# Rank-20 second phase of an attention and mixture-of-experts kernel: weight preparation rearranged

## The chip, the cores and the metric

The kernel runs on one core of one Trainium2 chip. The metric is the device time of one execution in microseconds, taken as the median of the runs. Five engines work side by side, each through its own instructions in order: PE (TensorE, the matrix multiplications), DVE (VectorE), ACT (ScalarE), POOL (GpSimd) and SP (SyncE, which here only issues transfers). Transfers issued by SP and by POOL run on the DMA engines.

## The reference

A linear attention with a complex decay makes `x`, and a dense mixture of four experts follows on it:

```python
for t in range(S):                     # S = 768; batch 4, heads 8, head_dim 48
    S_re, S_im = ar*S_re - ai*S_im + k_t v_t^T, ar*S_im + ai*S_re
    y[:, :, t] = q_t @ S_re
x = y as [3072, 384]
p = domain_probs / (domain_probs.sum(-1) + 1e-9)
for e in range(4):                     # w1[e]: 384x1024, w2[e]: 1024x384
    out += p[:, e:e+1] * (relu(x @ w1[e]) @ w2[e])
```

All of it is float32. The kernel reaches float32 accuracy on PE by splitting each operand into a high part and a low part (`hi`, `lo`, in the type fp32r) and taking three products, hi·hi, lo·hi and hi·lo.

## The kernel before

**First phase.** It does the attention in 12 groups of 256 tokens and, one group behind, the first two experts on them (`moe1`, lines 209 to 229). A step over two blocks of 128 hidden features does the first layer into `ph`, takes `hh` on ACT (L219) and `hl` on DVE (L220), and runs the second layer of the step before (`po`, L229). The attention's result goes to memory (`y_d`), the sum over the first two experts to `acc_d`. In the last group there is no attention left beside the matrix work; there the second phase's first operands are prepared.

**Second phase.** It does experts 2 and 3 (E1 = 2) on all tokens, with a first layer in a scheme of rank 20: a product of a 4x3 by a 3x2 grid of blocks in 20 block products in place of 24. There are 8 rounds R, four for each expert; a round takes 768 tokens, as two token blocks u of 384 in the scheme's columns. A round has two units h = 0 and 1, each for 4 of the expert's 8 feature blocks. A unit (`unit`, from the table `UNIT`) runs 20 products of three matmuls each (`M` rows, into PSUM banks `pb0` to `pb4`), with copies on ACT (`C`), sums on DVE (`D`) and the hidden activations' high and low parts (`H` on ACT, `L` on DVE). `SN` holds copies that those steps keep. At the 8 places marked `F` the unit calls `fill`, which runs nine matmuls of the second layer (`l2`, into `pob0` to `pob2`) for a token block that was finished before; so a full unit has 60 + 72 = 132 matmuls. At the places marked `B` it calls `bg(n)`, which takes n steps from the list `side`, in which the preparation of later operands waits. Each engine runs its instructions in the order in which they are written in the second phase (`pin`, `held`), the sums on POOL excepted; up to the first unit and for POOL's sums, the scheduler sets the order.

**Preparing x for a round** (`prep_x`): SP loads six blocks into `Z` slots 0 to 5 (`load_x2`, L1012), 12 sums are formed in `Z` slots 0 to 10 on POOL (`pool`, L895), the first five of them into slots 6 to 10, and each of 16 operands is split into `xh` on ACT (L886) and `xl` on DVE (L889 and L892).

**Preparing four feature blocks of an expert's weights** (`prep_w`): four loads of the first-layer weights into a staging area (L954), 15 sums of 128-column blocks on DVE (L889), splits into `shi` and `slo` tiles and `ext`, and for the second-layer weights a POOL transfer that writes the high part (L992), an ACT copy with sign turned and a POOL transfer that adds the weight onto it (L994). `late_w` says where this happens: the first half of expert 2 before the first unit, staged in `SN` with sums in `ACC`; the second half in unit (0, 0), and the two halves of expert 3 in the units (1, 0) and (4, 0), all three staged in `Z` slots 0 to 3, with sums in `Z` from slot 4 on. `side` holds the weights first, and the loads of x for the next round after them. At the end of a unit h = 0 all of `side` is emptied (`drain`).

`ACC` has two halves, one for each token block u; `acc_load` (L1085) brings the sum so far, L892 adds the round's result, and a POOL transfer (L1117) stores it, or an SP transfer (L1115) writes the output for the last expert.

Of the kernel before, what the change touches and what calls it, by code (L numbers as in the profile page):

```python
# [8 lines left out]
F32 = mybir.dt.float32  # L9
F32R = mybir.dt.float32r  # L10
AF = mybir.ActivationFunctionType
ALU = mybir.AluOpType
# [4 lines left out]
HD = H * D  # L17
NT = B * S
E, F = 4, 1024
P = 128  # L20
NJ = HD // P
# [6 lines left out]
FE = F // P  # L28
E1 = 2
# [20 lines left out]
TB2 = 384  # L50
C2 = TB2 // P
NB2 = NT // (2 * TB2)
# [46 lines left out]
def fast_path(ctx, tc, qkP, aP, vP, probsP, w, out, flag):  # L99
    nc = tc.nc  # L100
# [10 lines left out]
                            base=32, channel_multiplier=1)  # L111
# [24 lines left out]
    wts = {}  # L136
# [121 lines left out]
    mo = MoE()  # L258

    with ExitStack() as c1:  # L260
# [4 lines left out]
        def tmp(name):  # L265
# [6 lines left out]
                                base=0, channel_multiplier=-1)  # L272
# [70 lines left out]
        last = {}  # L343
# [66 lines left out]

        def pick(g, nm, X, dst, s, w):
            n = 4 if w == C else 3
# [367 lines left out]
        x = {}  # L780
# [79 lines left out]
    with ExitStack() as c2:  # L860
        fin = c2.enter_context(tc.tile_pool(name="fin", bufs=1))
        ps_b = c2.enter_context(tc.tile_pool(name="ps_b", bufs=1, space=PSUM))
        acc2_d = [dram.tile([P, HD], F32, name=f"acc2_d{c}") for c in range(NT // P)]
        NR2 = (E - E1) * NB2
        Z = fin.tile([P, 11 * TB2], F32, name="Z")
        SN = fin.tile([P, 7 * TB2], F32, name="SN")
        ACC = fin.tile([P, 2 * C2 * HD], F32, name="ACC")
        X = [tuple(fin.tile([P, TB2], F32R, name=f"x{nm}{n}") for nm in ("h", "l")) for n in range(16)]
        static, quads = {}, {}
        held = {"on": False}  # L870
        side, freed, ready = [], set(), set()
# [7 lines left out]
        def pin(ins):  # L879
            return tc.keep_in_program_order(ins) if held["on"] else ins  # L880
# [4 lines left out]
        def act(dst, src, fn=AF.Copy, scale=1.0):  # L885
            return pin(nc.scalar.activation(dst, src, fn, scale=scale))  # L886
# [27 lines left out]

        def step(*ops, need=None, on=None):
            f = tt if on is None else on

            def run():
                for o in ops:
                    f(*o)  # L920
            return ["sum" if on is None else "pool", need, run, None]
# [23 lines left out]
                second()  # L945
                n -= 1

        def prep_w(e, h, base, raw, sums):
            i = e * FE + 4 * h
            raw = raw.rearrange("p (f k c) -> p f k c", f=4, k=NJ)  # L950
            s = sums.rearrange("p (n c) -> p n c", c=P)

            def load(u):
                pin(nc.sync.dma_start(raw[:, u].rearrange("p k c -> p (k c)"), w[i + u][:, :HD]))  # L954

            hi, lo = ([slot(nm, base + n) for n in range(5)] for nm in ("hi", "lo"))
            ext = fin.tile([P, 4 * P], F32R, tag="ext", name=f"ext{i}", bufs=3)
            ops = {}
            for n, r in enumerate((12, 9, 7, 15, 6, 8, 1, 16, 14, 13, 17, 4, 3, 2, 10, 19, 11, 5)):
                ops[r] = hi[n // 6][:, cut(n % 6)], lo[n // 6][:, cut(n % 6)]  # L960
            ops[18], ops[0] = ((ext[:, cut(n)], ext[:, cut(2 + n)]) for n in range(2))
            quads[e, h] = ops

            def blocks(x, n):
                return x.rearrange("p (n c) -> p n c", c=P)[:, n]

            def a(f, k):
                return raw[:, f - 1, k - 1]

            def n(lo_, hi_):  # L970
                return s[:, lo_:hi_]

            add, sub = ALU.add, ALU.subtract
            out = [step(*[(u,) for u in range(4)], on=load), ["gap", None, 2, None],
                   step((n(0, 4), raw[:, :, 1], raw[:, :, 0], sub)),
                   step((n(10, 12), raw[:, 2, :2], raw[:, 3, :2], add), (s[:, 8], a(1, 3), a(4, 3), add)),
                   step((s[:, 9], a(2, 3), a(3, 3), add), (n(4, 6), n(0, 2), raw[:, :2, 2], add)),
                   step((n(6, 8), n(0, 2), n(8, 10), add), (s[:, 5], s[:, 5], a(4, 3), sub)),
                   step((s[:, 12], a(1, 2), a(2, 1), add), (s[:, 8], s[:, 12], s[:, 8], add),
                        (s[:, 9], s[:, 12], s[:, 9], sub)),  # L980
                   step((s[:, 10], s[:, 6], s[:, 10], sub), (s[:, 11], s[:, 7], s[:, 11], add)),
                   step((s[:, 13], a(3, 1), a(4, 2), add), (s[:, 14], a(3, 1), a(1, 2), sub))]
            for src, q, lim in ((n(0, 6), 0, slice(0, 6)), (n(6, 12), 1, slice(0, 6)), (n(12, 15), 2, slice(0, 3)),
                                (raw[:, 2, 0::2], 2, slice(3, 5)), (a(2, 1), 2, 5)):
                out.append(split(blocks(hi[q], lim), blocks(lo[q], lim), src))
            out.append(split(blocks(ext, slice(0, 2)), blocks(ext, slice(2, 4)), raw[:, 3, 1:3], mark=("w", e, h)))
            for u in range(4):
                d_hi, d_lo = (x[3 + u // 2][:, u % 2 * HD:(u % 2 + 1) * HD] for x in (hi, lo))
                wts[i + u] = d_hi, d_lo

                def minus(d_hi=d_hi, d_lo=d_lo, k=i + u):
                    nc.gpsimd.dma_start(d_hi, w[k][:, HD:])  # L992
                    act(d_lo, d_hi.bitcast(F32), scale=-1.0)
                    nc.gpsimd.dma_start(d_lo, w[k][:, HD:], accum_op=ALU.add)  # L994
                    if k == i + 3:
                        ready.add(("w2", e, h))
                out.append(["act", None, minus, None])
            return out

        def drain():  # L1000
            while side:
                bg(len(side))
# [157 lines left out]
        held["on"] = True  # L1160
        for R in range(NR2):
            for h in range(2):
                if h == 1 or R > 0:
                    acc_load(R if h == 1 else R - 1, 1 - h)
                if (R, h) in late_w:
                    e, q, base = late_w[R, h]
                    side += prep_w(e, q, base, Z[:, :4 * HD], Z[:, 4 * HD:4 * HD + 15 * P])
                if h == 0 and R + 1 < NR2:
                    todo_x = prep_x(R + 1)
                    side += todo_x[:2]  # L1170
                elif R + 1 < NR2:
                    freed.clear()
                    side += todo_x[2:]
# [205 lines left out]
```

## Time and profile before

| | |
|---|---|
| Median of 3 runs | 1015.28 us (1014.23 to 1017.97) |
| The profiled execution | 1014.26 us, of it 1012.6 us span |
| Granted TensorE clock, mean | 0.984 |
| PE busy | 958.2 us (95%) |
| DVE busy | 748.3 us (74%) |
| ACT busy | 479.3 us (47%) |
| POOL busy | 181.4 us (18%) |
| Second phase, first to last matmul | 604.46 to 1006.3 us |

A row of the timeline has the start, the length, the engine, line, operation, output and inputs, and in brackets how long the engine had been idle before it and what ended that. The matmuls of a row overlap a little, so the pace is read from their starts. In a table of windows each engine's column is its busy time in that stretch with the number of instructions in brackets, and PEclk is the mean granted clock. The profile has no chain of waits for this kernel, so the windows and the timeline take its place.

### The profile page before, as it was taken

The numbers are of one execution on the slowest core, as the hardware profiler recorded it, in microseconds if no ns is written. First come the engines' busy times: TensorE is split into PE (matmuls) and PEld (weight loads), VectorE is DVE, ScalarE is ACT, GpSimd is POOL, SyncE is SP. The second block draws the span as 40 slices with busy tenths as digits, with TensorE's granted clock in tenths as the row PEclk, the third lists the DMA queues.
The fourth block names the chain that finished last, engine by engine and source line by source line (L and its number), as shares of the span: only waits on it lengthen the run. The fifth ranks groups of instructions, "written<-read, shape, count | busy, mean of one in ns | idle before, by whom it ended". The sixth has DMA issues, their size and how long they took to land.

```text
span 1012.6 us, 17537 instructions
## 1 busy us (share of the span) xinstructions
PE 958.2 (95%) x6717; PEld 930.9 (92%) x6717; DVE 748.3 (74%) x1594; ACT 479.3 (47%) x952; POOL 181.4 (18%) x218
## 2 busy tenths in 40 slices
PE   5899999999999999999999897988999979999997
PEld 2799999999999999999999897888999969999997
DVE  7888989898988889798832656867575768475743
ACT  7756525546365363645422436544454535354430
POOL 6030000000000000000000433525333334223000
PEclk9999999999999999999999899998999999999999
DMA  9585277394784745648361345333313242231112
GB/s 300 177 179 127 76 188 162 100 217 100 181 181 136 188 124 150 173 110 198 85 133 48 94 109 129 109 80 95 119 51 107 78 107 74 94 94 49 48 47 74
DMA packets 107053, 123.82 MB, mean 122 GB/s; under 512 B 7440, under 2 KB 94528, under 8 KB 106960
## 3 DMA queue, kind: packets, MB, share of 16 engines
q1 hardware_dynamic: 95472, 95.69, 34.2%
q0 software_dynamic: 11488, 26.93, 11.7%
q8 instruction: 55, 0.90, 0.4%
q14 instruction: 38, 0.31, 0.1%
HBM read 81.96 MB, written 40.62 MB: 121 GB/s over the span
## 4 chain that ended last, share of the span: by engine, by line


## 5 line engine op out<-in xcount | busy, mean ns | idle before, releaser
L883 PE MATMUL pob<-shi,hid 128*128 128x384 f32 x528 | 149.7, 338 | 0.0
L229 PE MATMUL po<-whi,hh 128*128 128x384 f32 x384 | 130.0, 339 | 1.1 <-ACT hh L219 1.1
L229 PE MATMUL po<-whi,hl 128*128 128x384 f32 x384 | 125.3, 341 | 5.4 <-DVE hl L220 5.4
L219 ACT ACTIVATE hh<-ph 128x512 fp32r<-128x512 f32 x96 | 57.1, 595 | 153.4 <-PE ph L209 148.8
L229 PE MATMUL po<-wlo,hh 128*128 128x384 f32 x384 | 129.3, 337 | 0.0
L895 POOL TENSOR_TENSOR Z<-Z 128x384 f32<-128x384 f32 x96 | 105.4, 1122 | 123.0 <-DMA Z<-y_d 65.6
L883 PE MATMUL pb<-xh,shi 128*128 128x384 f32 x291 | 99.7, 344 | 22.8 <-ACT SN L886 13.5
L220 DVE SCALAR_TENSOR_TENSOR hl<-ph,hh 128x512 fp32r<-128x512 f32 x96 | 66.0, 688 | 53.7 <-ACT hh L219 53.0
L209 PE MATMUL ph<-xha,whi 128*128 128x256 f32 x576 | 104.3, 287 | 1.2 <-ACT xha L196 1.2
L209 PE MATMUL ph<-xha,wlo 128*128 128x256 f32 x576 | 101.8, 284 | 0.0
L209 PE MATMUL ph<-xla,whi 128*128 128x256 f32 x576 | 101.2, 284 | 0.4 <-DVE xla L198 0.4
L883 PEld LDWEIGHTS pob<-shi,hid 128*128 128x128 f32 x528 | 98.5, 192 | 0.0
L889 DVE TENSOR_TENSOR xl<-Z,xh 128x384 fp32r<-128x384 f32 x104 | 70.2, 705 | 37.7 <-ACT xh L886 32.1
L883 PE MATMUL pb<-xh,slo 128*128 128x384 f32 x288 | 97.9, 340 | 0.0
L883 PE MATMUL pb<-xl,shi 128*128 128x384 f32 x288 | 97.8, 340 | 0.0
L883 PE MATMUL pob<-slo,hid 128*128 128x384 f32 x264 | 89.3, 338 | 0.0
L209 PEld LDWEIGHTS ph<-xha,whi 128*128 128x128 f32 x576 | 86.5, 191 | 2.5 <-ACT xha L196 1.5
L209 PEld LDWEIGHTS ph<-xla,whi 128*128 128x128 f32 x576 | 82.9, 191 | 0.6 <-DVE xla L198 0.6
L209 PEld LDWEIGHTS ph<-xha,wlo 128*128 128x128 f32 x576 | 83.2, 191 | 0.2 <-issue 0.2
L883 PEld LDWEIGHTS pb<-xh,shi 128*128 128x128 f32 x291 | 55.5, 191 | 27.0 <-ACT SN L886 14.4
L229 PEld LDWEIGHTS po<-whi,hl 128*128 128x128 f32 x384 | 71.3, 189 | 7.0 <-DVE hl L220 6.9
L886 ACT ACTIVATE xh<-Z 128x384 fp32r<-128x384 f32 x128 | 60.6, 516 | 35.5 <-POOL Z L895 33.7
(217 smaller groups left out, 2069.1 us busy)
## 6 DMA issues: line engine op xcount, KB each, us to landing
qk<-qkP SPq DMA_DIRECT2D x24, 384.0 KB, 7.0
acc_d<-acc POOLq DMA_DIRECT2D x24, 384.0 KB, 4.8
ACC<-acc_d SPq DMA_DIRECT2D x48, 192.0 KB, 3.1
A<-aP SPq DMA_DIRECT2D x22, 384.0 KB, 8.0
Z<-y_d SPq DMA_DIRECT2D x16, 384.0 KB, 4.7
q_d<-Q SPq DMA_DIRECT2D x12, 387.0 KB, 3.9
Qst<-q_d SPq DMA_DIRECT2D x12, 387.0 KB, 5.8
v<-vP SPq DMA_DIRECT2D x24, 192.0 KB, 2.6
```

The source lines that it names most:

```text
L209: ins = nc.tensor.matmul(ph[:, u, :], wt[:, j * P:(j + 1) * P], xt[:, j, :], start=(n == 0), stop=(n == 3 * NJ - 1))
L219: wts["hh"] = nc.scalar.activation(hh, ph, AF.Relu)
L220: nc.vector.scalar_tensor_tensor(hl, ph, 0.0, hh, op0=ALU.max, op1=ALU.subtract)
L229: nc.tensor.matmul(po[t], ht[:, u, t * P:(t + 1) * P], wt[:, HD:], start=(i % FE == 0 and n == 0), stop=(i % FE == FE - 1 and n == 2))
L883: return tc.keep_in_program_order(nc.tensor.matmul(*args, **kw))
L886: return pin(nc.scalar.activation(dst, src, fn, scale=scale))
L889: pin(nc.vector.tensor_tensor(dst, x, y, op=op))
L895: nc.gpsimd.tensor_tensor(dst, x, y, op=op)
```

## The change

There is a tile of its own, `RX` (384 columns), and the staging areas are new. `prep_w` now returns its loads, its sums and splits, one step with the four W2 transfers that write the high parts ("casts"), and the four steps for their low parts ("tail") apart.

- Both halves of expert 2 are prepared before the first unit. The first is staged in the first half of `ACC` and in `RX`, the second in `SN`. The sums of both are formed in `Z` slots 6 to 10.
- The x sums of round 0 run on DVE in place of POOL.
- In units (1, 0) and (4, 0) the weights of expert 3 are staged in the first half of `ACC` and in `RX`, with sums in `Z` slots 6 to 10. Their loads are issued as the unit begins. The loads of x for the next round stand ahead of the weights in `side`, the five first x sums behind them, the tail in the unit h = 1.
- One second-layer step of the first token block moves from the end of the second unit to place 6 of the first, so the store of that block comes a step sooner.

```diff
-        def prep_w(e, h, base, raw, sums):
+        def prep_w(e, h, base, rows, last):
...
+            s = Z[:, 6 * TB2:].rearrange("p (n c) -> p n c", c=P)
...
             def a(f, k):
-                return raw[:, f - 1, k - 1]
+                return last[:, k - 1] if f == 4 else rows[:, f - 1, k - 1]
...
+            def loads():
+                for u in range(4):
+                    pin(nc.sync.dma_start(rows[:, u] if u < 3 else last,
+                                          w[i + u][:, :HD].rearrange("p (k c) -> p k c", k=NJ)))
...
-                def minus(d_hi=d_hi, d_lo=d_lo, k=i + u):
-                    nc.gpsimd.dma_start(d_hi, w[k][:, HD:])
-                    act(d_lo, d_hi.bitcast(F32), scale=-1.0)
-                    nc.gpsimd.dma_start(d_lo, w[k][:, HD:], accum_op=ALU.add)
...
+            def cast(k):
+                nc.gpsimd.dma_start(wts[k][0], w[k][:, HD:])
+
+            def rest(k):
+                act(wts[k][1], wts[k][0].bitcast(F32), scale=-1.0)
+                nc.gpsimd.dma_start(wts[k][1], w[k][:, HD:], accum_op=ALU.add)
...
             def g(*ops):
-                return step(*ops, on=pool)
+                return step(*ops, on=pool if R else None)
...
-        late_w = {(0, 0): (E1, 1, 5), (1, 0): (E1 + 1, 0, 10), (NB2, 0): (E1 + 1, 1, 0)}
+        half = C2 * HD
+        jobs = [prep_w(E1, h, 5 * h, x[:, :half], y) for h, x, y in ((0, ACC, RX), (1, SN, SN[:, half:half + HD]))]
         freed.update(range(16))
         side += prep_x(0)
-        drain()
-        side += prep_w(E1, 0, 0, SN[:, :4 * HD], ACC[:, :15 * P])
+        side[0][2]()
+        for job in jobs:
+            job[0]()
+        side.pop(0)
+        for _, main, casts, tail in jobs:
+            side += main + casts + tail
         drain()
...
+                if h == 0:
+                    side += todo_x[:1]
+                    tail = []
+                    if R in (1, NB2):
+                        loads, main, casts, tail = prep_w(E1 + 1, *((0, 10) if R == 1 else (1, 0)), ACC[:, :half], RX)
+                        loads()
+                        side += [["gap", None, 1, None]] + main + casts
+                    side += todo_x[1:2]
+                else:
+                    side += tail
...
-                def fill(k, first=(R == 0 and h == 0)):
-                    if not first:
+                def fill(k, u=2 * R + h):
+                    if u == 0 and k == 0:
+                        mo.flush()
+                    elif u > 1 or (u, k) == (0, 6) or (u == 1 and k < FE - 1):
                         l2()
-                    elif k == 0:
-                        mo.flush()
```

What this does to the order, at the three places that the prediction speaks of. First DVE in the last group of the first phase, between the low parts `hl_0` and `hl_1` of its first two steps, before:

```order
L220 SCALAR_TENSOR_TENSOR hl_0_6504<-ph_0_6484,hh_0_6503 128x512
L889 TENSOR_TENSOR xl_6825<-Z,xh_6824 128x384
L889 TENSOR_TENSOR xl_6827<-Z,xh_6826 128x384
L889 TENSOR_TENSOR xl_6831<-Z,xh_6830 128x384
L889 TENSOR_TENSOR ACC<-SN 128x128
L889 TENSOR_TENSOR xl_6843<-Z,xh_6842 128x384
L889 TENSOR_TENSOR xl_6821<-Z,xh_6820 128x384
L889 TENSOR_TENSOR ACC<-SN 128x128 x2
```

and after:

```order
L220 SCALAR_TENSOR_TENSOR hl_0_6504<-ph_0_6484,hh_0_6503 128x512
L890 TENSOR_TENSOR Z<-Z 128x384 x2
L890 TENSOR_TENSOR xl_6826<-Z,xh_6825 128x384
L890 TENSOR_TENSOR xl_6828<-Z,xh_6827 128x384
L890 TENSOR_TENSOR Z<-Z 128x384 x3
L890 TENSOR_TENSOR xl_6832<-Z,xh_6831 128x384
L890 TENSOR_TENSOR xl_6844<-Z,xh_6843 128x384
L893 SCALAR_TENSOR_TENSOR xl_6834<-Z,xh_6833 128x384
L890 TENSOR_TENSOR Z<-Z 128x384
L890 TENSOR_TENSOR xl_6822<-Z,xh_6821 128x384
L893 SCALAR_TENSOR_TENSOR xl_6816<-Z,xh_6815 128x384
L220 SCALAR_TENSOR_TENSOR hl_1_6545<-ph_1_6525,hh_1_6544 128x512
```

Weight sums (`ACC<-SN`) have left this stretch, and six x sums (`Z<-Z`) have come into it.

Second, ACT from the last high part of the first phase (`hh_7`) into the first unit, before; `acc` takes the last result of the first phase out of `po`, `pb<-pb` and `SN<-pb` are the unit's first copies:

```order
L219 ACTIVATE hh_7_6760<-ph_7_6741 128x512
L886 ACTIVATE pb_6960<-pb_6956 128x384
L682 ACTIVATE acc_1_6979<-po_4_0_6669,pr 128x384
L682 ACTIVATE acc_1_6979<-po_4_1_6670,pr 128x384
L886 ACTIVATE SN<-pb_6956 128x384
```

and after:

```order
L219 ACTIVATE hh_7_6760<-ph_7_6741 128x512
L887 ACTIVATE shi_6856<-Z 128x768
L887 ACTIVATE shi_6857<-Z 128x768
L887 ACTIVATE shi_6858<-Z 128x384
L887 ACTIVATE shi_6858<-SN 128x256
L887 ACTIVATE shi_6858<-SN 128x128
L682 ACTIVATE acc_1_7024<-po_4_0_6669,pr 128x384
L887 ACTIVATE slo_6864<-shi_6859 128x384
L682 ACTIVATE acc_1_7024<-po_4_1_6670,pr 128x384
L887 ACTIVATE slo_6864<-shi_6859 128x384
L887 ACTIVATE slo_6865<-shi_6860 128x384 x2
L887 ACTIVATE pb_7005<-pb_7001 128x384
```

The unit's first copy now stands behind the `acc` copies and four copies of the second weight half.

Third, POOL in round 1, from the store of the token block before to the x sums for round 2, before:

```order
L992 DMA shi_7356<-w 128x384 x2
L992 DMA shi_7357<-w 128x384 x2
L1117 DMA acc_d_6788<-ACC 128x384
L994 DMA slo_7361<-w 128x384 x2
L1117 DMA acc_d_6789<-ACC 128x384
L994 DMA slo_7362<-w 128x384
L1117 DMA acc_d_6790<-ACC 128x384
L994 DMA slo_7362<-w 128x384
L895 TENSOR_TENSOR Z<-Z 128x384 x12
```

and after:

```order
L993 DMA shi_7359<-w 128x384 x2
L993 DMA shi_7360<-w 128x384 x2
L896 TENSOR_TENSOR Z<-Z 128x384 x6
L1121 DMA acc_d_6788<-ACC 128x384
L1121 DMA acc_d_6789<-ACC 128x384
L1121 DMA acc_d_6790<-ACC 128x384
L997 DMA slo_7364<-w 128x384 x2
L997 DMA slo_7365<-w 128x384 x2
L896 TENSOR_TENSOR Z<-Z 128x384 x6
```

Six of the twelve sums now stand ahead of the block's store, in the unit h = 0, as they do in the rounds without weights. In round 4 the rows have the same shape.

More of the change, by code (lines that the diff above doesn't have):

```diff
@@ L867, in fast_path @@
         ACC = fin.tile([P, 2 * C2 * HD], F32, name="ACC")
+        RX = fin.tile([P, TB2], F32, name="RX")
         X = [tuple(fin.tile([P, TB2], F32R, name=f"x{nm}{n}") for nm in ("h", "l")) for n in range(16)]
@@ L946, in bg @@
                 n -= 1
-        def prep_w(e, h, base, raw, sums):
+        def prep_w(e, h, base, rows, last):
             i = e * FE + 4 * h
[L950 to L954, printed above, removed]
             hi, lo = ([slot(nm, base + n) for n in range(5)] for nm in ("hi", "lo"))
             ext = fin.tile([P, 4 * P], F32R, tag="ext", name=f"ext{i}", bufs=3)
+            rows = rows.rearrange("p (f k c) -> p f k c", f=3, k=NJ)
+            last = last.rearrange("p (k c) -> p k c", k=NJ)
+            s = Z[:, 6 * TB2:].rearrange("p (n c) -> p n c", c=P)
             ops = {}
@@ L967, in a @@
             def a(f, k):
-                return raw[:, f - 1, k - 1]
+                return last[:, k - 1] if f == 4 else rows[:, f - 1, k - 1]
             def n(lo_, hi_):
                 return s[:, lo_:hi_]
+            def loads():
+                for u in range(4):
+                    pin(nc.sync.dma_start(rows[:, u] if u < 3 else last,
+                                          w[i + u][:, :HD].rearrange("p (k c) -> p k c", k=NJ)))
             add, sub = ALU.add, ALU.subtract
[L974 to L977, printed above, removed]
+            out = [step((n(0, 3), rows[:, :, 1], rows[:, :, 0], sub), (s[:, 3], a(4, 2), a(4, 1), sub)),
+                   step((n(10, 12), rows[:, 2, :2], last[:, :2], add), (s[:, 8], a(1, 3), a(4, 3), add)),
+                   step((s[:, 9], a(2, 3), a(3, 3), add), (n(4, 6), n(0, 2), rows[:, :2, 2], add)),
                    step((n(6, 8), n(0, 2), n(8, 10), add), (s[:, 5], s[:, 5], a(4, 3), sub)),
@@ L983, in prep_w @@
             for src, q, lim in ((n(0, 6), 0, slice(0, 6)), (n(6, 12), 1, slice(0, 6)), (n(12, 15), 2, slice(0, 3)),
-                                (raw[:, 2, 0::2], 2, slice(3, 5)), (a(2, 1), 2, 5)):
+                                (rows[:, 2, 0::2], 2, slice(3, 5)), (a(2, 1), 2, 5)):
                 out.append(split(blocks(hi[q], lim), blocks(lo[q], lim), src))
-            out.append(split(blocks(ext, slice(0, 2)), blocks(ext, slice(2, 4)), raw[:, 3, 1:3], mark=("w", e, h)))
+            out.append(split(blocks(ext, slice(0, 2)), blocks(ext, slice(2, 4)), last[:, 1:], mark=("w", e, h)))
             for u in range(4):
-                d_hi, d_lo = (x[3 + u // 2][:, u % 2 * HD:(u % 2 + 1) * HD] for x in (hi, lo))
-                wts[i + u] = d_hi, d_lo
-                def minus(d_hi=d_hi, d_lo=d_lo, k=i + u):
-                    nc.gpsimd.dma_start(d_hi, w[k][:, HD:])
-                    act(d_lo, d_hi.bitcast(F32), scale=-1.0)
-                    nc.gpsimd.dma_start(d_lo, w[k][:, HD:], accum_op=ALU.add)
[L995 to L998, printed above, removed]
+                wts[i + u] = tuple(x[3 + u // 2][:, u % 2 * HD:(u % 2 + 1) * HD] for x in (hi, lo))
+            def cast(k):
[3 more added lines that the diff above has]
+                nc.gpsimd.dma_start(wts[k][1], w[k][:, HD:], accum_op=ALU.add)
+                if k == i + 3:
+                    ready.add(("w2", e, h))
+            ks = [(i + u,) for u in range(4)]
+            return loads, out, [step(*ks, on=cast)], [["act", None, lambda k=k: rest(*k), None] for k in ks]
         def drain():
@@ L1152, in unit @@
                     bg(op[1])
-        late_w = {(0, 0): (E1, 1, 5), (1, 0): (E1 + 1, 0, 10), (NB2, 0): (E1 + 1, 1, 0)}
+        half = C2 * HD
+        jobs = [prep_w(E1, h, 5 * h, x[:, :half], y) for h, x, y in ((0, ACC, RX), (1, SN, SN[:, half:half + HD]))]
         freed.update(range(16))
         side += prep_x(0)
-        drain()
-        side += prep_w(E1, 0, 0, SN[:, :4 * HD], ACC[:, :15 * P])
+        side[0][2]()
[4 more added lines that the diff above has]
+            side += main + casts + tail
         drain()
         held["on"] = True
+        todo_x = []
         for R in range(NR2):
@@ L1164, in fast_path @@
                     acc_load(R if h == 1 else R - 1, 1 - h)
[L1165 to L1173, printed above, removed]
-                def fill(k, first=(R == 0 and h == 0)):
-                    if not first:
-                        l2()
-                    elif k == 0:
-                        mo.flush()
+                todo_x = prep_x(R + 1) if h == 0 and R + 1 < NR2 else todo_x
+                if R + 1 == NR2:
+                    todo_x = []
+                if h == 0:
[8 more added lines that the diff above has]
+                    side += tail
+                    if R + 1 < NR2:
+                        freed.clear()
+                        side += todo_x[2:]
+                def fill(k, u=2 * R + h):
+                    if u == 0 and k == 0:
+                        mo.flush()
+                    elif u > 1 or (u, k) == (0, 6) or (u == 1 and k < FE - 1):
+                        l2()
                 unit(R, h, fill)
```

## The prediction

> **What bounds the kernel now.** I read the busy shares first, then the slices, then PE in windows, and last the timeline of each engine at the places where PE falls short.
>
> ```profile
> PE 958.2 (95%) x6717; PEld 930.9 (92%) x6717; DVE 748.3 (74%) x1594; ACT 479.3 (47%) x952; POOL 181.4 (18%) x218
> PE   5899999999999999999999897988999979999997
> PEclk9999999999999999999999899998999999999999
> ```
>
> PE is the bound over the whole span. Its slices fall below 9 at the start, which the change doesn't touch, in slices 23 to 28, and once more in slice 33. The windows give the size (busy time, matmuls in brackets, granted clock):
>
> ```profile
> 565.00:604.46 39.46, 34.51 (x223) 0.91 0.51 123
> 604.46:650.00 45.54, 37.87 (x199) 0.96 0.39 96
> 650.00:700.00 50.00, 43.09 (x231) 0.90 0.42 119
> 700.00:815.00 115.00, 115.00 (x664) 1.00 0.26 82
> 815.00:850.00 35.00, 26.82 (x139) 0.90 0.35 91
> 850.00:1000.00 150.00, 150.00 (x867) 1.00 0.23 72
> ```
>
> The stretches 700 to 815 and 850 to 1000 are rounds without weight preparation: PE never waits, at 867/150 = 5.78 matmuls per us. A window's loss is its length less its matmuls at that pace: round 0 (604 to 650) 45.5 - 199/5.78 = 11.1 us, round 1 (650 to 700) 50 - 231/5.78 = 10.0, round 4 (815 to 850) 35 - 139/5.78 = 11.0. The end of the first phase has matmuls of two sizes, so there I take the waits and the slow clock:
>
> ```profile
> 578.60 1.01 PE L229 MATMUL po<-whi,hl 128*128 128x384 f32 x2 [4.32 <-DVE hl L220]
> 585.91 0.62 PE L229 MATMUL po<-whi,hl 128*128 128x384 f32 x2 [0.63 <-DVE hl L220]
> 578.60:583.30 4.70, 4.70 (x18) 4.70 (x19) 4.70 (x5) 2.10 (x4) 4.70 (x5) 0.50 0.00 0
> ```
>
> 4.32 + 0.63 us of waits, and 4.7 us at a granted clock of 0.50, which cost 2.35: 7.3 us. All four together are 39.4 us. Nothing more is to be had from this change: the floor is 1014.3 - 39.4 = 974.9.
>
> **Where the losses come from.** In rounds 1 and 4 it is one chain:
>
> ```profile
> 677.51 2.08 SPq L1012 DMA_DIRECT2D Z<-y_d x4
> 685.09 1.94 POOL L895 TENSOR_TENSOR Z<-Z 128x384 f32<-128x384 f32 x2 [4.15 <-issue]
> 686.11 0.52 ACT L886 ACTIVATE xh<-Z 128x384 fp32r<-128x384 f32 x1 [8.63 <-POOL Z L895]
> 687.07 0.69 PE L883 MATMUL pb<-xh,shi 128*128 128x384 f32 x1 [6.63 <-ACT SN L886]
> 825.19 2.28 SPq L1012 DMA_DIRECT2D Z<-y_d x4
> 835.03 0.69 PE L883 MATMUL pb<-xh,shi 128*128 128x384 f32 x1 [6.92 <-ACT SN L886]
> ```
>
> The weights sit in the `Z` slots of x. So the loads of x start only after the weights' last split (677.51), the first sum on POOL starts at 685.09, and ACT stands 8.63 us before the `xh` that needs it. The unit's own copy `SN` is queued behind that `xh`, and PE waits 6.63 us for it, then runs slowly. Round 4 repeats it.
>
> In round 0 the preparation of the second weight half sits on DVE in a unit without second-layer matmuls to hide it:
>
> ```profile
> 616.82 0.44 PE L883 MATMUL pb<-xh,shi 128*128 128x384 f32 x1 [1.16 <-DVE pb L889]
> 621.34 0.44 PE L883 MATMUL pb<-xh,shi 128*128 128x384 f32 x1 [2.17 <-DVE pb L889]
> 623.60 0.44 PE L883 MATMUL pb<-xh,shi 128*128 128x384 f32 x1 [1.45 <-DVE pb L889]
> 624.40:628.00 3.60, 3.60 (x13) 3.60 (x13) 1.54 (x4) 2.15 (x6) 1.80 (x2) 0.53 0.83 213
> 643.66 0.44 PE L883 MATMUL pb<-xh,shi 128*128 128x384 f32 x1 [1.42 <-DVE pb L889]
> ```
>
> And in the first phase's last group DVE itself is slow while POOL adds:
>
> ```profile
> 577.82 7.02 POOL L895 TENSOR_TENSOR Z<-Z 128x384 f32<-128x384 f32 x6 [2.52 <-DVE xl L892]
> 581.45 1.36 DVE L889 TENSOR_TENSOR xl<-Z,xh 128x384 fp32r<-128x384 f32 x1
> 586.85 0.55 DVE L889 TENSOR_TENSOR xl<-Z,xh 128x384 fp32r<-128x384 f32 x1
> 587.32 0.48 DVE L889 TENSOR_TENSOR ACC<-ACC 128x128 f32<-128x128 f32 x2
> ```
>
> The same split takes 1.36 us beside POOL's sums and 0.55 without them, and then the next operation starts 0.47 us after it (586.85 to 587.32).
>
> **The change, part by part.** *Round 1 and round 4.* The loads of x leave the chain: slots 0 to 5 are free during the whole unit h = 0. What remains is that the first five sums go to slots 6 to 10, which now hold the weights' sums. A slot is free when its split's `slo` has run:
>
> ```profile
> 670.25 0.96 DVE L889 TENSOR_TENSOR slo<-Z,shi 128x768 fp32r<-128x768 f32 x1 [0.46 <-ACT shi L886]
> 677.37 0.42 DVE L889 TENSOR_TENSOR ext<-Z,ext 128x256 fp32r<-128x256 f32 x1
> ```
>
> So the first sum can start near 671 in place of 685, 14 us sooner, and its `xh` is ready when ACT gets there. The chain's waits of 6.63 and 6.92 us and the slow stretch behind them go. What comes late next is DVE. It is busy without a break from 670 to 678, and POOL's six sums now fall into those 8 us. By 1.36 against 0.55 us, six splits could each be held up by 0.8 us, 4.8 us in all, and the next unit's first `pb` sum is queued behind them. Against that, the weights' sums start one place `B` sooner (gap 1, not 2). I take 2 us of remaining loss in each round, between 0 (the later rounds, where POOL adds in h = 0 without a wait of PE) and 7 (4.8 us of wait and 2.35 of slow clock): nearer to the later rounds, since PE's own slack of nine-matmul steps is the same.
>
> [...]
>
> *The new staging area* must be free in time: the store of the block before, then the weight loads, then the sums.
>
> ```profile
> 798.81 1.64 POOL L1117 DMA_DIRECT2D acc_d<-ACC x3 [8.61 <-DVE ACC L892]
> acc_d<-ACC POOLq DMA_DIRECT2D x24, 192.0 KB, 2.4
> Z<-w SPq DMA_DIRECT2D x12, 192.0 KB, 3.6
> 806.22 0.56 DVE L892 SCALAR_TENSOR_TENSOR hidhl<-pb,hidhh 128x384 fp32r<-128x384 f32 x1 [2.40 <-ACT hidhh L886]
> 808.82 0.55 DVE L889 TENSOR_TENSOR SN<-SN,pb 128x384 f32<-128x384 f32 x1 [2.04 <-PE pb L883]
> ```
>
> The store's last issue ends at 800.45, it lands at 802.9 and the load behind it at 806.5. DVE reaches the sums after the row of 806.22, at 806.8, and was idle for 2.04 us there. The load is on time by 0.3 us; a delay of 2 us would still lie in the idle time. In round 1 the moved second-layer step makes the store sooner by nine matmuls (9/5.78 = 1.6 us). I cost it at nothing; if a load came 3 us late, 1 us a round. The moved step itself changes no count of matmuls. The low parts of W2 go a unit later; in round 4 they are due at the fifth second-layer step of (4, 1), some 13 us into the unit (13 products and 4 steps are 75 matmuls), and are queued behind six sums and a store that end some 5 us into it. Their price is nothing.
>
> *Round 0.* The second half's sums and splits leave unit (0, 0) for the end of the first phase, and five x sums of round 1 go to POOL in (0, 0) rather than after it. The waits of 1.16, 2.17 and 1.45 us shrink to what the unit's own sums cost without second-layer work, some 0.7 us, with one step at place 6 to fill. There is a new wait. The unit's first `pb` copy stood ahead of the `acc` copies and now stands behind them and four `slo` copies:
>
> ```profile
> 592.80 0.93 ACT L886 ACTIVATE slo<-shi 128x384 fp32r<-128x384 f32 x2
> 605.36 0.47 ACT L886 ACTIVATE pb<-pb 128x384 f32<-128x384 f32 x1 [2.18 <-PE pb L883]
> 607.43 1.10 ACT L682 ACTIVATE acc<-po,pr 128x384 f32<-128x384 f32 x2 [1.60 <-PE po L229]
> ```
>
> From the first `acc` on that is 1.10 + 2 x 0.93 + 0.47 = 3.4 us; PE has three matmuls left at that point, 3/5.78 = 0.5 us, so it waits some 2.9 us for the bank that the copy reads. Does this wait slow the clock? The row of 624.40 to 628 shows 0.53 after waits of 2.17 and 1.45 us close together, and the single 1.42 at 643.66 was followed by none. I take it, 3.6 us at half: 1.8. Round 0 then loses 2.9 + 1.8 + 0.7 = 5.4 in place of 11.1. The bounds are 2 and 9.
>
> [...]
>
> *The end of the first phase.* POOL adds nothing there any more: the splits take 0.55 instead of 1.36. DVE takes the 12 sums, and the second half's 15 sums and 6 splits besides. The sums need the second half of x:
>
> ```profile
> 569.85 3.61 POOL L895 TENSOR_TENSOR Z<-Z 128x384 f32<-128x384 f32 x3 [0.47 <-DMA Z<-y_d]
> 598.98 0.69 DVE L220 SCALAR_TENSOR_TENSOR hl<-ph,hh 128x512 fp32r<-128x512 f32 x1 [3.54 <-ACT hh L219]
> 603.21 0.69 DVE L220 SCALAR_TENSOR_TENSOR hl<-ph,hh 128x512 fp32r<-128x512 f32 x1 [3.54 <-ACT hh L219]
> ```
>
> From 569.85 on, DVE has 12 operations ahead of `hl_1`, a new one each 0.47 us: `hl_1` starts at 575.5 and ends at 576.2, and PE waits from 578.60 - 4.32 = 574.3 on. That is 1.9 us in place of 4.32. The later stretches between two `hl` hold 2 to 4.7 us of work at 0.47 us for an operation on 384 columns and about half for one on 128, against a step of PE of 603.21 - 598.98 = 4.23 us. I take 2.5 us for this end, between 0 and 7.3: the extra DVE work may keep the old loss.
>
> **The sum.** 2.5 + 5.4 + 2 + 2 = 11.9 us of loss in place of 39.4, a gain of 27.5: 1014.3 - 27.5 = 986.8 for an execution like the profiled one. The median was 1.0 us above that one, so I predict 988.
>
> **Rivals.** [...] POOL's sums beside the weights' splits cost the full 7 us in rounds 1 and 4, and the first phase's end keeps 5: 12.5 more than the forecast, 1000. For it speaks 1.36 against 0.55, and DVE's full 8 us; against it the rounds that run POOL in h = 0 without a wait. *The waits only move.* If x is late by another way, as with the sums' last reader `ext` at 677.8 instead of the first `slo`, the loss of rounds 1 and 4 stays at 16 of 21 us: 988 + 12 = 1000 too; with all four losses kept, no change, 1015. *Slower.* DVE in the last group becomes the bound: a step of PE is 4.23 us, and beyond it each of the seven low parts would be late by what DVE has more. To be slower than before by 5 us, those steps must lose 32 us more than the 2.5 forecast, 4.6 each, so DVE would need 8.8 us between two `hl`, where I count 4.7 at most. That gives 1020, and little speaks for it.
>
> **Chances.** The forecast 0.72 (its own range 980 to 995), half kept 0.22 (995 to 1006), no change 0.03, slower 0.03. Outside 979 to 999 lie the last two and the upper part of the second, about 2 in 10. A change of 0.5%, 5 us, is about what can be told from none: faster 0.94, same 0.03, slower 0.03.
>
> **What would show it.** Right: no wait of PE above 3 us past 610, and PE's loss in rounds 1 and 4 under 4 us each; POOL's first sum for round 2 before the unit (1, 1) begins; DVE's splits at 0.55 in the last group; PE waiting 2.5 to 3.5 us for ACT's first `pb` copy. Wrong: splits at 1.36 with PE waiting on DVE at the turn of rounds 1 and 4, DVE idle for a weight load into `ACC` or `RX`, or PE waiting on several `hl`.

## The result and the profile after

The changed kernel takes 990.69 us (median of four runs, 986.92 to 991.16), against 1014.75 for the kernel before in the same session (1013.84 to 1017.97): a ratio of 0.9749, 95% interval 0.9717 to 0.9782. Run again with the first experiments it took 988.02 (987.13 to 991.43), ratio 0.9737 [0.9713, 0.9761]. The four runs of the changed kernel lie 4.2 us apart at granted clocks of 0.992 to 0.994, and the profiled one is the fastest of them (986.92). Part of such differences lies in the first phase: over the profiled executions of all the kernels here, the first load of x for the second phase is issued anywhere from 561.20 to 564.20 us. So kernels are compared by ratio, and stages by the profiled executions: 1014.26 before, 986.92 after, 27.3 us, where the medians are 24.1 apart (28.0 in the second session).

The page of the changed kernel, first its busy shares, then two rows of its slices:

```profile
PE 951.1 (97%) x6717; PEld 924.6 (94%) x6717; DVE 752.5 (76%) x1610; ACT 480.0 (49%) x952; POOL 168.4 (17%) x206
PE   5899998999999999999999998999999999999997
PEclk9999999999999999999999998999999999999999
```

Of the slices 23 to 28 and 33, which held five figures below 9 before, only slice 25 still falls short, just where the second phase starts. PE in windows of the changed kernel (length, busy time with matmuls in brackets, clock, DMA share, GB/s):

```profile
596.07:650.00 53.93, 48.48 (x259) 0.94 0.46 103
650.00:700.00 50.00, 48.58 (x277) 1.00 0.40 110
700.00:800.00 100.00, 100.00 (x579) 1.00 0.27 85
800.00:850.00 50.00, 48.46 (x277) 1.00 0.32 83
```

At the pace of the third row, 5.79 matmuls per us, round 0 (first row) loses 53.93 - 259/5.79 = 9.2 us, rounds 1 and 4 lose 50 - 277/5.79 = 2.2 each. The timeline of PE in the changed kernel has these waits, the row of a window behind them:

```profile
573.40 0.62 PE L229 MATMUL po<-whi,hl 128*128 128x384 f32 x2 [0.45 <-DVE hl L220]
604.08 0.69 PE L884 MATMUL pb<-xh,shi 128*128 128x384 f32 x1 [4.55 <-ACT pb L887]
635.32 0.62 PE L884 MATMUL pob<-shi,hid 128*128 128x384 f32 x2 [0.60 <-DVE hid L893]
681.35 0.44 PE L884 MATMUL pb<-xh,shi 128*128 128x384 f32 x1 [1.16 <-DVE pb L890]
821.02 0.44 PE L884 MATMUL pb<-xh,shi 128*128 128x384 f32 x1 [1.16 <-DVE pb L890]
604.08:608.00 3.92, 3.92 (x12) 0.50 1.02 125
```

The waits of 6.63 and 6.92 us at the turn of rounds 1 and 4 are gone; the largest left there are 1.16 each, on another row. The wait of 4.32 for `hl` has become 0.45. One large wait is left, and it is new: 4.55 us for ACT's first copy of `pb` in unit (0, 0), with 3.9 us at half clock behind it, 6.5 us together. The timelines of POOL and of ACT ahead of it show what it is made of:

```profile
592.34 3.59 POOL L997 DMA_DIRECT2D slo<-w x4 [5.18 <-ACT slo L887]
594.56 3.54 POOL L993 DMA_DIRECT2D shi<-w x4
```

```profile
599.04 0.58 ACT L682 ACTIVATE acc<-po,pr 128x384 f32<-128x384 f32 x1 [1.53 <-PE po L229]
601.42 0.52 ACT L887 ACTIVATE slo<-shi 128x384 fp32r<-128x384 f32 x1 [1.80 <-DMA shi<-w]
601.85 0.56 ACT L682 ACTIVATE acc<-po,pr 128x384 f32<-128x384 f32 x1
602.31 1.33 ACT L887 ACTIVATE slo<-shi 128x384 fp32r<-128x384 f32 x3
603.55 0.47 ACT L887 ACTIVATE pb<-pb 128x384 f32<-128x384 f32 x1
```

POOL's transfers of W2's high parts for the second half are issued from 594.56 to 598.1, behind those of the first half's low parts. ACT stands at its first `slo` copy until 601.42, 1.80 us idle, for one of them to land. Three `slo` copies and the `pb` copy follow without a gap. Why the transfer lands only 3.3 us after the last issue isn't shown: over the whole kernel, a `shi<-w` transfer took 5.9 us from issue to landing (median of 16), and 3.1 in the kernel before.

In round 1, SP, POOL and DVE of the changed kernel:

```profile
642.20 1.74 SPq L973 DMA_DIRECT2D ACC<-w x3
644.99 2.12 SPq L1016 DMA_DIRECT2D Z<-y_d x4
```

```profile
657.01 7.28 POOL L896 TENSOR_TENSOR Z<-Z 128x384 f32<-128x384 f32 x6 [13.24 <-DVE slo L890]
673.12 7.29 POOL L896 TENSOR_TENSOR Z<-Z 128x384 f32<-128x384 f32 x6 [1.43 <-DVE xl L890]
```

```profile
649.17 0.56 DVE L890 TENSOR_TENSOR Z<-ACC 128x384 f32<-128x384 f32 x1 [0.39 <-DMA ACC<-w]
670.28 0.56 DVE L890 TENSOR_TENSOR xl<-Z,xh 128x384 fp32r<-128x384 f32 x1 [2.53 <-ACT xh L887]
672.86 0.55 DVE L893 SCALAR_TENSOR_TENSOR xl<-Z,xh 128x384 fp32r<-128x384 f32 x1
673.33 1.38 DVE L890 TENSOR_TENSOR xl<-Z,xh 128x384 fp32r<-128x384 f32 x1
674.62 0.54 DVE L890 TENSOR_TENSOR SN<-SN,pb 128x384 f32<-128x384 f32 x1
675.56 2.70 DVE L893 SCALAR_TENSOR_TENSOR xl<-Z,xh 128x384 fp32r<-128x384 f32 x2
678.18 2.65 DVE L890 TENSOR_TENSOR xl<-Z,xh 128x384 fp32r<-128x384 f32 x2
```

The loads of x are issued at 644.99 instead of 677.51, and POOL's first sum is at 657.01, before the unit (1, 1). The first six sums delay nothing at the turn to the unit (1, 1): DVE is idle for 2.53 us before 670.28. The second six stretch DVE's splits of x from 0.55 to 1.38 us; a sum that reads `pb`, in PSUM, takes 0.54 in the middle of that stretch.

### The profile page after: what moved, and what is told of

It reads as the page before. It is cut to its first block, busy times and chain, and to the rows that moved or that the text cites. A ratio compares the mean times of both kernels' runs of the same rounds, so it can differ in the third digit from the quotient of the medians.

```text
span 985.2 us, 17543 instructions
## 1 busy us (share of the span) xinstructions
PE 951.1 (97%) x6717; PEld 924.6 (94%) x6717; DVE 752.5 (76%) x1610; ACT 480.0 (49%) x952; POOL 168.4 (17%) x206
## 4 chain that ended last, share of the span: by engine, by line
## 5 line engine op out<-in xcount | busy, mean ns | idle before, releaser
L896 POOL TENSOR_TENSOR Z<-Z 128x384 f32<-128x384 f32 x84 | 95.5, 1195 | 127.8 <-DVE xl L890 54.5
L884 PEld LDWEIGHTS pob<-shi,hid 128*128 128x128 f32 x528 | 96.4, 188 | 2.4 <-DVE hid L893 1.2
L890 DVE TENSOR_TENSOR xl<-Z,xh 128x384 fp32r<-128x384 f32 x104 | 63.4, 638 | 21.9 <-ACT xh L887 14.3
L887 ACT ACTIVATE SN<-pb 128x384 f32<-128x384 f32 x96 | 47.2, 492 | 65.7 <-PE pb L884 58.3
L229 PEld LDWEIGHTS po<-whi,hh 128*128 128x128 f32 x384 | 72.4, 189 | 1.5 <-ACT hh L219 1.3
L887 ACT ACTIVATE hid<-pb 128x384 fp32r<-128x384 f32 x76 | 37.3, 490 | 72.9 <-PE pb L884 72.5
```

The lines of the kernel that those rows point to most:

```text
L229: nc.tensor.matmul(po[t], ht[:, u, t * P:(t + 1) * P], wt[:, HD:], start=(i % FE == 0 and n == 0), stop=(i % FE == FE - 1 and n == 2))
L884: return tc.keep_in_program_order(nc.tensor.matmul(*args, **kw))
L890: pin(nc.vector.tensor_tensor(dst, x, y, op=op))
L896: nc.gpsimd.tensor_tensor(dst, x, y, op=op)
```

## The experiments

**What is the wait of 4.55 us worth, and is it ACT's queue?** Two kernels move the low parts of W2 for the second half (four ACT copies and four POOL transfers).

*tail_mid*: the low parts go into the middle of unit (0, 0).

```diff
-        for _, main, casts, tail in jobs:
-            side += main + casts + tail
+        side += jobs[0][1] + jobs[0][2] + jobs[0][3] + jobs[1][1] + jobs[1][2]
...
                     side += todo_x[1:2]
+                    if R == 0:
+                        side += [["gap", None, 3, None]] + jobs[1][3]
```

> The low parts of W2 of expert 2's second half (four ACT copies and four POOL transfers) are taken in the middle of unit (0, 0), not ahead of it. Theory A: PE's 4.55 us wait and the 3.9 us at half clock in the first unit (1.96 us) exist only because ACT's first pb copy stands behind those four copies, which wait for the transfers of the high parts. Then the wait falls to 1 us or less and the slow stretch goes: 990.7 - 5.5 = 985, ratio 0.970. Theory B: the first unit has nothing from the second layer to fill it, and PE would wait there anyway, for the copies of the first phase's last result or for DVE; the wait only moves, 990 to 991.

Measured: 981.74 us, ratio 0.9667 [0.9642, 0.9692], beside 0.9737 [0.9713, 0.9761] for the changed kernel on the same chip. Its PE and ACT:

```profile
608.17 0.44 PE L884 MATMUL pb<-xh,shi 128*128 128x384 f32 x1 [0.53 <-ACT SN L887]
676.08 0.44 PE L884 MATMUL pb<-xh,shi 128*128 128x384 f32 x1 [1.17 <-DVE pb L890]
```

```profile
598.28 0.47 ACT L887 ACTIVATE pb<-pb 128x384 f32<-128x384 f32 x1
599.91 1.11 ACT L682 ACTIVATE acc<-po,pr 128x384 f32<-128x384 f32 x2 [1.16 <-PE po L229]
```

The `pb` copy runs ahead of the `acc` copies, and no wait of PE between 600 and 650 is above 0.6 us. The kernel is 988.02 - 981.74 = 6.3 us faster than the changed one; 4.55 of wait and 3.92/2 of half clock are 6.5. So the four copies and the transfers that they wait for are the cause. (The expected time was counted from 990.7, and the changed kernel itself took 2.7 us less beside these runs; the expected gain was 5.5.)

*tail_later*: the same low parts at the first place of unit (0, 0) instead of its middle (`side += todo_x[:1] + jobs[1][3]`, with no gap).

> The same low parts, but at the first place for side work of unit (0, 0), right behind the first pb copy. Theory A: that copy is free, and PE gets as far as the first SN copy; the four copies ahead of it still wait for the transfers until some 5 us into the unit, so PE waits 2 to 3 us there: 988.5, ratio 0.973, between the changed kernel and the version with the copies in the middle. Theory B: as the changed kernel, 990 to 991. If what matters were only that the copies are out of the first phase, it would be as fast as the version in the middle, 985.

Measured: 984.85 us, ratio 0.9697 [0.9677, 0.9717]. One wait remains, on the unit's next copy:

```profile
602.58 0.45 PE L884 MATMUL pb<-xh,shi 128*128 128x384 f32 x1 [2.00 <-ACT SN L887]
602.50:606.50 4.00, 3.92 (x15) 0.65 0.86 128
```

The wait is as expected, the time 3.6 us better, of which 2.5 are the changed kernel's own time beside it, 988.02 for the 990.5 expected.

*after_again*, the changed kernel itself beside these:

> The changed kernel once more, as the reference for the runs beside it. One execution of it took 986.9 us and three took 990.4 to 991.2, so I expect a median of 990.5 with single runs down to 987, ratio to the kernel before 0.975. Both theories say the same of this one; what it adds is how far single executions lie apart.

Its wait of PE is 4.15 us, on the same copy.

**Does the moved second-layer step matter?** *fill_old* puts it back.

```diff
-                    elif u > 1 or (u, k) == (0, 6) or (u == 1 and k < FE - 1):
+                    elif u > 0:
```

> The changed kernel with the second-layer steps where they were before: none in the first unit, all eight in the second. Theory A: the step at place 6 hides about 1.5 us of the first unit's own waits, and the store of the first token block comes 1.6 us later, which the weight loads of unit (1, 0) can still take: 992, ratio 0.977. Rival: the moved step has no effect, since the first unit's time is set by ACT's late start: 990.7.

Measured: 988.23 us, ratio 0.9729 [0.9706, 0.9752], the same as after_again. Two waits of 0.55 and 0.82 us come into unit (0, 0), too little to measure. That this step brings the store forward was worth nothing that can be seen.

**The parts alone.** *late_only* has only what concerns rounds 1 and 4; round 0 is prepared as before (second half staged in `Z`, its x sums on POOL), and the second-layer steps stand where they were.

> Only the part of the change in rounds 1 and 4: the weights of expert 3 in their own staging, casts early, low parts a unit later; round 0 and the end of the first phase as before. Theory A: the losses of rounds 1 and 4 fall from 10.0 and 11.0 us to 2.2 each, nothing else changes: 1014.7 - 16.6 = 998, ratio 0.984, and PE waits of over 3 us remain only near 575. Rival: the losses of the rounds hang together with round 0 (a late start of round 1's x is passed on to round 2), then less: 1003 to 1008.

Measured: 999.04 us, ratio 0.9843 [0.9821, 0.9865], as the first theory has it. Its PE keeps the waits of the kernel before in the last group and in round 0 (one row of each):

```profile
577.33 0.62 PE L229 MATMUL po<-whi,hl 128*128 128x384 f32 x2 [4.19 <-DVE hl L220]
620.22 0.44 PE L884 MATMUL pb<-xh,shi 128*128 128x384 f32 x1 [2.14 <-DVE pb L890]
```

*only_x0_dve* is the kernel before with only round 0's x sums on DVE (`on=pool if R else None`).

> The kernel before with one line changed: the 12 x sums of round 0 on DVE. Theory A: DVE's splits in the last group of the first phase took 1.36 us only beside POOL's sums; without them PE's 4.32 us wait and the half clock behind it go, though DVE has 12 more operations: 1014.7 - 6 = 1009, ratio 0.994. Rival: DVE is the late engine there because it has too much to do, and 12 more operations make it later: 1015 to 1019.

Measured: 1009.77 us, ratio 0.994 [0.9921, 0.996]. The wait for `hl` falls from 4.32 to 2.30 us:

```profile
576.01 0.62 PE L229 MATMUL po<-whi,hl 128*128 128x384 f32 x2 [2.30 <-DVE hl L220]
576.00:580.00 4.00, 3.99 (x17) 0.59 0.19 51
```

The direction and the time are the first theory's, the wait only in part: it halves, and a slow stretch stays behind it. The weights' sums are still in that stretch here; whether they are what keeps the rest was not tried alone.

*half2_in_unit* is the changed kernel with the second weight half prepared in unit (0, 0), staged in the second half of `ACC` and in `RX`.

```diff
-        jobs = [prep_w(E1, h, 5 * h, x[:, :half], y) for h, x, y in ((0, ACC, RX), (1, SN, SN[:, half:half + HD]))]
+        jobs = [prep_w(E1, h, 5 * h, x[:, :half], y) for h, x, y in ((0, SN, SN[:, half:half + HD]),)]
...
-                    if R in (1, NB2):
+                    if R in (0, 1, NB2):
```

> The changed kernel, but expert 2's second half is prepared in unit (0, 0) again, now staged in the second half of ACC and in RX. Theory A: ACT's late first copy is gone (-6.5 us), and the waits on DVE in the first unit come back, some 3 to 5 us: 988, ratio 0.973, and PE waits on DVE near 612 to 622. Rival: those waits came from the staging in Z, not from DVE's work, and now are gone too: 984.

Measured: 988.32 us, ratio 0.9728 [0.9706, 0.9749], no different from the changed kernel, but by other waits:

```profile
610.58 0.44 PE L884 MATMUL pb<-xh,shi 128*128 128x384 f32 x1 [1.65 <-DVE pb L890]
617.32 0.44 PE L884 MATMUL pb<-xh,shi 128*128 128x384 f32 x1 [2.29 <-DVE pb L890]
634.36 0.44 PE L884 MATMUL pb<-xh,shi 128*128 128x384 f32 x1 [1.16 <-DVE pb L890]
```

As the change is built, taking the second half out of unit (0, 0) exchanges DVE's waits there for ACT's one; only with the low parts moved on does it pay.

**Round 0's x sums: DVE or POOL?** *x0_on_pool* is the changed kernel with them back on POOL.

```diff
-                return step(*ops, on=pool if R else None)
+                return step(*ops, on=pool)
```

> The changed kernel with the x sums of round 0 back on POOL. Theory A: splits at 1.36 us again in the last group, now with the preparation of both weight halves on DVE: PE waits on the low parts as before or longer: 990.7 + 7 = 998, ratio 0.983. Rival: the gain of that stretch came from the weights' sums leaving it, and POOL's sums cost nothing: 990 to 992.

Measured: 989.51 us, ratio 0.9738 [0.9718, 0.9758]: no change that can be told, the rival's time. But the mechanism of the first theory is there. PE, its windows, and DVE:

```profile
576.09 0.62 PE L229 MATMUL po<-whi,hl 128*128 128x384 f32 x2 [2.23 <-DVE hl L220]
583.46 0.44 PE L229 MATMUL po<-whi,hl 128*128 128x384 f32 x1 [3.19 <-DVE hl L220]
607.74 0.44 PE L884 MATMUL pb<-xh,shi 128*128 128x384 f32 x1 [1.77 <-ACT pb L887]
583.40:587.40 4.00, 3.94 (x28) 1.00 0.79 200
607.70:612.00 4.30, 4.26 (x17) 0.67 0.98 149
```

```profile
566.84 6.26 DVE L890 TENSOR_TENSOR xl<-Z,xh 128x384 fp32r<-128x384 f32 x5 [0.79 <-DMA Z<-y_d]
```

Splits take 1.25 us again, and the waits for `hl` cost 2.23 + 3.19 - 0.45 = 5.0 us more. In return PE comes to the `pb` copy later, and the wait there with its slow clock is 1.77 + 4.3 x 0.33 = 3.2 instead of 6.5. PE comes to the copy 6.4 us later (607.74 - 1.77, for 604.08 - 4.55), and the copy is ready only 3.7 us later (607.74 for 604.08). In ACT's timeline one of POOL's transfers of W2, and not DVE, is what the copy's queue waits for (4.02 us, until 605.30). So the one wait eats part of the other. That predicts that the sums' place counts as soon as the copy is no longer late:

*mid_x0_pool* makes the same edit in tail_mid.

> The kernel tail_mid (second half's low parts of W2 taken in the middle of unit (0,0)), with round 0's six x sums of the last group put back on GpSimd. A (in the changed kernel these sums cost nothing on GpSimd only because the wait for ScalarE's copy of pb hid them; here that wait is gone): hl waits of TensorE near 2.2 and 3.2 us come back and nothing takes them up, 987 us, ratio about 0.972. B (the place of the sums is worth nothing in any kernel with the own staging area): 982, ratio about 0.967, as tail_mid.

Measured: 988.62 us, ratio 0.974 [0.9724, 0.9755], against 0.9667 [0.9642, 0.9692] for tail_mid.

```profile
577.75 0.62 PE L229 MATMUL po<-whi,hl 128*128 128x384 f32 x2 [2.07 <-DVE hl L220]
585.11 0.69 PE L229 MATMUL po<-whi,hl 128*128 128x384 f32 x1 [3.17 <-DVE hl L220]
585.10:589.00 3.90, 3.89 (x13) 0.50 0.63 131
```

2.07 + 3.17 + 3.9/2 = 7.2 us, and 981.74 + 7.2 = 988.9. The sums on DVE are worth 7 us where nothing else is late, and nothing in the changed kernel as it stands.

**The remaining 1.16 us in rounds 1 and 4.** *mid_no_sums* leaves out POOL's x sums of rounds 2 and 5; the edit to tail_mid is `step(*(() if R in (2, 5) else ops), ...)`. (24 operations in all, 12 for each round, where the expectation counts 12.)

> tail_mid with GpSimd's sums of x for rounds 2 and 5 left out (all twelve operations; the rounds' low-rank factors are then not those of the reference). A (the 1.17 us waits for DVE's copy of pb in units (1,1) and (4,1) come from DVE's splits running beside GpSimd's sums): both waits are gone or below 0.3 us and the splits of rounds 2 and 5 there take about 0.55 us instead of 1.3, time 979 to 981. B (the waits come from the order on DVE alone): they stay at 1.1 to 1.2 us, time as tail_mid, 980 to 982.

Measured, one run: 975.76 us, below the 979 to 981 of the first theory; how far that goes beyond the scatter, one run can't say. No wait of PE is left in the units (1, 1) and (4, 1), and the splits are short (DVE):

```profile
672.14 1.02 DVE L890 TENSOR_TENSOR xl<-Z,xh 128x384 fp32r<-128x384 f32 x2
```

*mid_x25_dve* computes these sums, on DVE: tail_mid with `on=None if R in (0, 2, 5) else pool`. (Again 24 operations.)

> tail_mid with the x sums of rounds 2 and 5 on VectorE as well as round 0's. A (twelve more operations of about 0.55 us on DVE, against splits that no longer stretch): the 1.17 us waits go, DVE is no later than before, 980 us, ratio 0.9655. B (DVE is late with hid or with the copies of pb): waits of 1 to 2 us in units (1,0) to (2,0), 984, ratio 0.969.

Measured: 977.98 us (976.71 to 980.45), ratio 0.9646 [0.9631, 0.9661], the fastest of the kernels that do the whole computation. Its page, and PE in its windows:

```profile
PE 946.3 (97%) x6717; PEld 920.5 (94%) x6717; DVE 749.3 (77%) x1634; ACT 480.0 (49%) x952; POOL 139.8 (14%) x182
```

```profile
650.00:700.00 50.00, 49.68 (x285) 1.00 0.35 96
800.00:850.00 50.00, 50.00 (x290) 1.00 0.33 91
```

The 1.17 us waits are gone. DVE runs 24 operations more than in tail_mid (1634 against 1610) and is busy 749.3 us for 751.1 there: without these sums it was 739.0 (mid_no_sums), so what they add on DVE, 10.3 us, is no more than the 12.1 us by which it had been longer with POOL's. Rounds 1 and 4 gain (285 - 277 + 290 - 277)/5.79 = 3.6 us on the changed kernel. The intervals of this kernel and of tail_mid overlap (they ran in different sessions); between their profiled executions these two windows account for 3.5 us (277 and 278 matmuls in tail_mid), and their medians are 3.8 apart.

**Is the unit's grace for the low parts worth anything?** *tail_same_unit* takes them in the same unit in rounds 1 and 4.

```diff
-                        side += [["gap", None, 1, None]] + main + casts
+                        side += [["gap", None, 1, None]] + main + casts + tail
+                        tail = []
```

> The changed kernel with W2's low parts of rounds 1 and 4 taken in the same unit as their high parts, instead of a unit later. A (with the own staging area on time, the later place of the low parts is worth nothing): 988 to 991, ratio 0.9735, no new wait above 1 us in units (1,0) and (4,0). B (the unit's grace is what brings the gain in these rounds): waits for DVE or for GpSimd's transfers return, 993 or more, ratio 0.978.

Measured: 986.09 us, ratio 0.9724 [0.9708, 0.9739], no slower than the changed kernel. Its PE waits just under 1 us at a new place, and less at the old one:

```profile
665.27 0.44 PE L884 MATMUL pob<-shi,hid 128*128 128x384 f32 x1 [0.98 <-DVE ACC L893]
680.45 0.44 PE L884 MATMUL pb<-xh,shi 128*128 128x384 f32 x1 [0.35 <-DVE pb L890]
```

## Why the prediction was right

The time, 988 forecast and 990.7 measured (988.0 when run again), and the places are right; two terms were mis-sized in opposite directions, and one came out right by another row than the one forecast.

- **Rounds 1 and 4** were forecast at 2 us each and lose 2.2. The chain from the weights' last split over the loads of x is cut as described; POOL's first sum, forecast near 671, came at 657.01. late_only has this part alone and gains some 16 us. That the 2 us fit is in part luck. They were put on the weights' splits beside POOL's first six sums, with the next unit's first `pb` sum queued behind them. Nothing is late there: DVE is idle for 2.53 us before 670.28, and PE has no wait above 0.25 us at that turn. What is late is a `pb` sum inside the unit (1, 1), behind five splits of x beside the second six sums: they stretch by 0.8 us each, 4 us together, of which PE waits 1.16. So the price of POOL's sums beside the splits, which the first rival (half kept) puts at the full 7 us in each of these rounds, is there, but beside other splits and at another place, and most of it falls into slack of DVE. mid_no_sums and mid_x25_dve confirm the cause of that 1.16.
- **The end of the first phase** was forecast at 2.5 and loses 0.45. The step "DVE has 12 operations ahead of `hl_1`" was too pessimistic: of the 13 operations between `hl_0` and `hl_1`, DVE of the changed kernel runs four before the second part of x lands and nine after it (from 568.44 to the `hl` at 572.66), and 3 x 0.47 us are 1.4 of the 2 us of difference. The splits are 0.55 us, as forecast, and mid_x0_pool shows that the sums' place is why. Of the rival by which DVE becomes the bound there, no later `hl` shows a wait.
- **Round 0** was forecast at 5.4. Its waits and its slow clock are 4.55 + 1.96 + 0.60 = 7.1 (9.2 by the pace, which also counts gaps too short to be listed here). The wait for the first `pb` copy was forecast at its place, 2.9 us by the length of ACT's queue, and measures 4.55, above the 2.5 to 3.5 that were named as a sign. The term left out what that queue itself waits for: 1.80 us for POOL's transfer of `shi`. The slow clock behind it, 1.8, is 1.96. The second layer's step in place 6 hides what was costed to it (fill_old: 0.55 and 0.82 us without it).
- **Costed at nothing**: the staging area was late by 0.39 us in round 1 and not at all in round 4; the low parts' place and the moved step are nothing by tail_same_unit and fill_old. PE shows no wait for the staging area, and all three hold.
- **The sum**: 0.45 + 9.2 + 2.2 + 2.2 = 14.1 us by the forecast's own measure, for 11.9. That is 39.4 - 14.1 = 25.3 of the 27.3 us between the two profiled executions. Some 1.3 of the other 2 us arise in the first phase ahead of the change: the first load of x for the second phase is issued at 562.80 before and at 561.48 after. That is no effect of the change that can be told, since the same kernel profiled again issues it at 562.11; so it is partly chance that 27.3 comes so near the 27.5 forecast.

## What to carry to other kernels

When work is moved ahead of a phase, follow the queue of each engine over the seam, and for each row in it ask what that row waits for: ACT's queue was counted right here, and the transfer that its first `slo` copy waits for was not. The wait and its slow clock cost 6.5 us where 4.7 were forecast, and a later place for eight instructions gave them back. GpSimd's sums had a price on VectorE here, 1.38 us for a split beside them against 0.55 without (changed kernel, round 1): 24 of them were better placed on VectorE (977.98 against 981.74 us, 3.5 us of it in the two windows), which became no busier with more to do (749.3 against 751.1 us). Two waits on one path can hide each other, as x0_on_pool and mid_x0_pool show, so an edit that measures as nothing should be tried again once the larger wait is gone.

## What the runs showed of the hardware

*The clock after short waits.* The granted clock fell to 0.50 behind waits of PE of 4.55 us (changed kernel, 604.08 to 608.00) and 4.15 us (after_again, 603.88 to 607.88), but it also fell to 0.67 behind one of 1.77 (x0_on_pool, 607.70 to 612.00), to 0.65 behind one of 2.00 (tail_later, 602.50 to 606.50) and to 0.59 behind one of 2.30 (only_x0_dve, 576.00 to 580.00). It stayed at 1.00 in x0_on_pool behind 2.23 (576.00 to 580.00) and 3.19 (583.40 to 587.40); in mid_x0_pool 3.17 at the same place brought it to 0.50 (585.10 to 589.00). Behind 2.29 in half2_in_unit (617.32) the matmuls start some 0.17 us apart from 617.60 on, the pace of the undisturbed rounds (1/5.79). So the length of the wait alone doesn't decide. Nor does the slow stretch begin where the wait ends: in tail_later PE resumes at 602.58, its matmuls start some 0.17 us apart from 602.87 to 603.56, and 0.32 us apart from 603.75 to 606.95. A wait of some 2 us therefore cost between 2.1 (2.07 in mid_x0_pool, with a clock of 1.00 from 577.70 to 581.00) and 3.9 here (2.30 + 4 x 0.41).

*VectorE beside GpSimd.* A split of x on 384 columns took 1.25 us (x0_on_pool, mean of the five from 566.84 on) to 1.38 us (changed kernel, 673.33) beside GpSimd's sums and 0.55 without them (changed kernel, 672.86), and a sum with an operand in PSUM amid them took 0.54 (changed kernel, 674.62).
